# Softmax weights that leave PSUM before they are split, with reciprocals, padded values and matmul order rearranged

## The chip, the cores and the metric

The kernel runs on one core of a Trainium2 chip. The metric is the device time of one execution in microseconds (us). Three runs of the kernel before gave 1035.32 (median), 1034.66 and 1037.95 us.

Engines are named as the profile names them: PE (TensorE, matmuls), PEld (its weight loads), DVE (VectorE), ACT (ScalarE), POOL (GpSimd) and SP (SyncE, which here issues DMAs). Each takes its instructions in one fixed order.

## The reference, cut to what matters

Attention over 8 batches, 12 heads, 448 positions, 64 channels, followed by a gated MLP per batch with a spatial matmul over positions:

```python
q_n, k_n = rmsnorm(q, g_q), rmsnorm(k, g_k)
scores = q_n @ k_n.T / 8
attn = exp(scores - max(scores))
attn = attn / (sum(attn) + 1e-9)
x = attn @ v                          # (8, 448, 768) after merging heads
h = gelu_tanh(x @ w_in)               # 768 -> 1024, w_in and w_out are float64
u, v = h[..., :512], h[..., 512:]
v_n = (v - mean(v)) / sqrt(var(v) + 1e-6) * g_ln
v_s = einsum('ts,bsd->btd', w_sg, v_n) + b_sg[None, :, None]
out = x + (u * v_s) @ w_out
```

## The kernel before, in words

To keep float32 accuracy on float16 matmuls, most operands are split into a high and a low part: the high part is a cast, the low part the value less the cast, and a product takes three matmuls (high by high, low by high, high by low).

**Turns.** The program is written as 48 turns, one for a pair of heads (i; six of them make a batch b). Two pairs form a unit u. In a unit, `scores(u)` handles seven tiles of 128 query rows for two heads each. For a tile: matmuls into a PSUM buffer `s` (L389, two buffers of two banks, `ps_s`), the negated row maximum on DVE (`nm`, L392), two exponentials on ACT in place in PSUM, which also write the row sums (L394), a copy to float16 on ACT (`ahl`, L397), the low part by a subtraction on DVE that reads PSUM and the copy (L398), and a DMA transpose into `at` (L403), the softmax weights with keys on partitions. The `s` buffer is free for the scores two tiles later when the subtraction is done. `ahl` has three buffers.

**One turn behind**, `pv(i)` makes the output of a pair: `recips(i)` forms the reciprocals of the row sums (add on POOL L413, reciprocal on DVE L414, cast to `rh` and low part `rl` on POOL L415 and L416), spreads them over partitions with 16 small matmuls (`row`, L423) and copies them out of PSUM (L426). Then 24 matmuls multiply `v` (split by `vsplit` on ACT and DVE, L369 and L370) with `at` (L446), in three pieces between which other work is put. 448 positions are 3.5 tiles of 128, so the fourth tile of a head fills half of the partitions; both heads of a pair share it, and its matmuls run as 64-by-64 tiles of PE's array. The output is scaled (L450) and split into `xh` and `xl` (L453, L454).

**MLP.** `moe(b)` is a generator that the turns of the next batch advance: the matmuls for the `v` half (L510, L513), the gelu, the layer norm, the `u` half (L568), the spatial matmul (L598: for each of four 128-column pieces f, nine matmuls over full tiles and three over the half tile, whose rows lie on one half of the partitions for f 0 and 1 and on the other for f 2 and 3), the gate (DVE L603, POOL L604, L607, L608), and the output matmuls (L632, L636, L638, L644). Weights are decoded from float64 in the first two batches' turns (L152 to L158, L241 to L247).

**POOL** also normalises and splits q and k of the units ahead (L329, L330, L335).

**What sets the order.** Streams (scores, pv, weights, moe) are interleaved by shares: in a turn `scores` gets SC steps, `pv` SV steps, `moe` its M steps, each step being the code up to the next `yield`. On top of that the framework's scheduler places the instructions of each engine by priority and by its own simulated time line, so that the built order is not the written one.

Of the kernel before, what the change touches and what calls it, by code (L numbers as in the profile page):

```python
# [34 lines left out]
SC, SV = 7, 4  # L35
# [11 lines left out]
def kernel(  # L47
# [236 lines left out]
    VR = {}  # L284

    def load_v(i):
# [6 lines left out]
        vr = ld.tile([P, GV, C7, D], F32, name="vr", bufs=NVR)  # L293
# [2 lines left out]
        for h, half, s0, c0, n in ((0, lo, 0, 0, C4), (0, hi, 0, C4, CM), (1, lo, C4, C4, CM), (1, hi, CM, 0, C4)):
# [76 lines left out]
    at_all = att.tile([P, 2 * C7, NAT * S], F16, name="at", bufs=1)  # L373

    def scores(u):
# [5 lines left out]
        for t in range(C7):  # L381
# [10 lines left out]
            V.tensor_reduce(out=nm, in_=ps[:, :, 0:S], axis=AX.X, op=ALU.max, negate=True)  # L392
            for h in range(2):
                A.activation(out=ps[:, h, 0:S], in_=ps[:, h, 0:S], func=AF.Exp, bias=nm[:, h:h + 1], accum_out=sums[:, t, h:h + 1])  # L394
# [2 lines left out]
            A.activation(out=ahl[:, 0], in_=ps[:, :, 0:S], func=AF.Copy)  # L397
            V.tensor_tensor(out=ahl[:, 1], in0=ps[:, :, 0:S], in1=ahl[:, 0], op=ALU.subtract)  # L398
# [7 lines left out]
    def recips(i):  # L406

        u, j = divmod(i, NG)
        cs = slice(0, C4) if j == 0 else slice(CM, C7)
# [3 lines left out]
        G.tensor_scalar(out=x, in0=sums, scalar1=1e-9, scalar2=None, op0=ALU.add)  # L413
# [1 line left out]
        G.tensor_copy(out=rh, in_=y)  # L415
        G.tensor_tensor(out=rl, in0=y, in1=rh, op=ALU.subtract)  # L416
        ps = ps_v.tile([P, 512], F32, name="row", tag="pv")[:, 0:S]
        for n, t in enumerate(range(cs.start, cs.stop)):
            ks, o = (slice(0, P), t * P - j * S) if t != CM else ((lo, SM), (hi, 0))[j]
            for rx in (rh, rl):  # L420
                for h in range(2):
                    w = ks.stop - ks.start
                    mm(out=ps[h * HP:(h + 1) * HP, o:o + w], lhsT=rx[ks, 2 * n + h:2 * n + h + 1].broadcast_to([w, HP]),  # L423
                       rhs=ident_h[ks, ks], start=(n == 0 and rx is rh), stop=(n == CM and rx is rl), skip_group_check=True)
# [6 lines left out]
    def pv(i):  # L431
# [12 lines left out]
        for k_, (vx, n, hx) in enumerate(blocks):  # L444
# [347 lines left out]
```

## Time and profile before

| | |
|---|---|
| median of 3 runs | 1035.32 us (1034.66 to 1037.95) |
| profiled execution, span | 1033.44 us, 1031.6 us |
| mean granted clock of PE | 0.916 |
| DMA moved | 155.70 MB, queue q1 69.0% of 16 engines |
| scores (L389) | 1152 matmuls in 168 tiles |
| subtractions (L398) | 168, 182.1 us of DVE |
| spatial matmuls (L598) | 384, of which 96 over half of the rows |

Busy shares are averages over stretches with different limits, so the stretches are read one by one: to 250 us the weights are decoded beside the first turns, from 250 to 960 us attention and MLP run together, and the last 72 us hold the last MLP alone. A wait row reads "engine, tile and line that waited, the one that ended the wait: us in total, times, longest".

### The profile page before, as it was taken

To read this page: it belongs to the slowest core of one execution; us is meant where nothing else is said; L and a number is where in the kernel's file an instruction comes from. 1 tells how busy PE (TensorE), PEld (TensorE's weight loads), DVE (VectorE), ACT (ScalarE), POOL (GpSimd) and SP (SyncE) were. 2 spreads that over 40 slices of the span, in tenths; PEclk is the share of its full clock that TensorE was granted. 3 is DMA by queue.
4 is the path that set the end of the run, shared out by engine and by line. 5 is a ranking of instruction groups with operands and counts; after the bars stand their busy time and mean duration, and the time that the engine had idled before them with its cause. 6 is when DMAs were issued, how large, how long until landed. Compare 5 with 4: busy or idle time off the path is not lost.

```text
span 1031.6 us, 16639 instructions
## 1 busy us (share of the span) xinstructions
PE 829.0 (80%) x5844; PEld 421.1 (41%) x5844; DVE 733.3 (71%) x1332; ACT 738.1 (72%) x1449; POOL 386.9 (38%) x403
## 2 busy tenths in 40 slices
PE   0243666858798997899689998999779998998798
PEld 0111222324444563346234553446324563454246
DVE  6698888999587667786677758786669666766230
ACT  3767779877868767777768767987777776877351
POOL 1468614567253505243251606341533414030021
PEclk9976687969899999999699998999889999999899
DMA  6998748776886398478886488959967676556102
GB/s 163 214 228 191 166 115 196 185 176 130 181 197 150 88 204 180 98 170 145 186 175 147 99 194 183 182 123 176 194 142 160 141 166 125 106 135 123 40 1 62
DMA packets 448004, 155.70 MB, mean 151 GB/s; under 512 B 404336, under 2 KB 441776, under 8 KB 447920
## 3 DMA queue, kind: packets, MB, share of 16 engines
q1 hardware_dynamic: 447344, 154.18, 69.0%
q8 instruction: 46, 0.75, 0.3%
q10 hardware_dynamic: 576, 0.46, 0.2%
q14 instruction: 38, 0.31, 0.1%
HBM read 43.57 MB, written 11.01 MB: 53 GB/s over the span
## 4 chain that ended last, share of the span: by engine, by line
PE 34%; DVE 21%; ACT 19%; DMA 11%; issue 8%; SPq 4%; POOL 4%; ACTq 0%; POOLq 0%; DVEq 0%
PE pv L446 6%; ACT s L394 5%; DVE ahl L398 5%; PE s L389 4%; DVE nm L392 3%; ACT ahl L397 2%; DMA vr<-in_v_dram 2%; ACT sqk L308 2%; DMA raw<-in_moe_w_in_dram 2%; DMA at<-ahl 2%; POOL qk L330 2%; DMA qt<-hl 2%; DMA qk<-in_k_dram 2%; ACT hl L334 2%; SPq L336 1%
## 5 line engine op out<-in xcount | busy, mean ns | idle before, releaser
L394 ACT ACTIVATE s<-s,nm 128x448 f32<-128x448 f32 x336 | 204.0, 607 | 109.8 <-DVE nm L392 106.8
L398 DVE TENSOR_TENSOR ahl<-s,ahl 128x896 f16<-128x896 f32 x168 | 182.1, 1085 | 100.8 <-ACT ahl L397 99.8
L389 PE MATMUL s<-qt 64*128 64x448 f16 (+1 forms) x1152 | 143.2, 390 | 110.7 <-DVE ahl L398 76.4
L392 DVE TENSOR_REDUCE nm<-s 128x2 f32<-128x896 f32 x168 | 180.8, 1082 | 40.5 <-PE s L389 40.0
L397 ACT ACTIVATE ahl<-s 128x896 f16<-128x896 f32 x168 | 153.4, 920 | 5.3 <-DMA at<-ahl 3.1
L446 PE MATMUL pv<-at,vh 128*64 128x448 f16 (+1 forms) x768 | 122.7, 398 | 16.4 <-DMA at<-ahl 7.6
L413 POOL TENSOR_SCALAR rx<-sums 128x8 f32<-128x8 f32 x48 | 13.4, 278 | 311.8 <-ACT s L394 310.4
L389 PEld LDWEIGHTS <-qt 64*128 64x128 f16 (+1 forms) x1152 | 45.3, 102 | 177.2 <-issue 135.9
L330 POOL TENSOR_TENSOR qk<-qk,ny 128x896 f32<-128x896 f32 x46 | 80.8, 1774 | 85.8 <-DVE ny L125 82.3
L335 POOL TENSOR_TENSOR hl<-qk,hl 128x896 f16<-128x896 f32 x46 | 87.7, 1917 | 55.1 <-ACT hl L334 54.5
L568 PEld LDWEIGHTS <-wi 128*128 128x128 f16 x576 | 55.9, 100 | 60.2 <-issue 14.1
L446 PEld LDWEIGHTS <-vh 128*64 128x64 f16 (+1 forms) x768 | 43.4, 117 | 84.3 <-issue 70.2
L309 DVE TENSOR_REDUCE ss<-sqk 128x14 f32<-128x896 f32 x48 | 51.8, 1080 | 29.2 <-ACT sqk L308 28.9
L394 ACT ACTIVATION_READ_ACCUMULATOR s<-s,nm 128x1 f32 x336 | 67.7, 201 | 0.0
L329 POOL TENSOR_TENSOR qk<-qk,gg 128x896 f32<-128x896 f32 x23 | 48.0, 2085 | 43.2 <-ACT sqk L308 39.3
L423 PE MATMUL row<-ident_h,rh 128*64 128x128 f16 (+1 forms) x384 | 36.7, 240 | 31.7 <-POOL rh L415 24.0
L604 POOL TENSOR_TENSOR gt<-gt,u 128x448 f32<-128x448 f32 x32 | 38.5, 1206 | 60.1 <-DVE gt L603 55.9
L446 PE MATMUL pv<-at,vl 128*64 128x448 f16 (+1 forms) x384 | 60.4, 394 | 0.0
L334 ACT ACTIVATE hl<-qk 128x896 f16<-128x896 f32 x48 | 44.9, 947 | 15.9 <-POOL qk L330 8.4
L308 ACT ACTIVATE sqk<-qk 128x896 f32<-128x896 f32 x48 | 45.6, 951 | 8.2 <-DVE ss L309 4.4
L510 PEld LDWEIGHTS <-xh 128*128 128x128 f16 x288 | 27.0, 101 | 49.2 <-issue 21.9
L369 ACT ACTIVATE vh<-vr,v_s 128x448 f16<-128x448 f32 x48 | 31.9, 668 | 19.7 <-PE pv L446 19.6
(996 smaller groups left out, 1960.8 us busy)
## 6 DMA issues: line engine op xcount, KB each, us to landing
out_dram<-ot SPq DMA_DIRECT2D x56, 192.0 KB, 2.9
vr<-in_v_dram SPq DMA_DIRECT2D x32, 192.0 KB, 3.3
raw<-in_moe_w_in_dram SPq DMA_DIRECT2D x12, 512.0 KB, 5.7
qk<-in_q_dram SPq DMA_DIRECT2D x47, 128.0 KB, 2.8
qk<-in_k_dram SPq DMA_DIRECT2D x47, 128.0 KB, 2.8
vr<-in_v_dram SPq DMA_DIRECT2D x32, 144.0 KB, 3.3
qk<-in_q_dram SPq DMA_DIRECT2D x47, 96.0 KB, 2.6
qk<-in_k_dram SPq DMA_DIRECT2D x47, 96.0 KB, 2.6
```

Of the source, the lines that this page charges most:

```text
L308: A.activation(out=skv, in_=U[u]["qk"][:, x].rearrange("p h c d -> p (h c) d"), func=AF.Square)
L309: V.tensor_reduce(out=SS[u][:, x], in_=skv, axis=AX.X, op=ALU.add)
L330: E.tensor_tensor(out=qk, in0=qk, in1=r["rs"][:, x * SSW:(x + 1) * SSW].unsqueeze(2).broadcast_to([P, SSW, D]), op=ALU.mult)
L334: A.activation(out=h_, in_=r["qk"][:, x], func=AF.Copy)
L335: E.tensor_tensor(out=l_, in0=r["qk"][:, x], in1=h_, op=ALU.subtract)
L389: mm(out=ps[r_, h, 0:S], lhsT=qt[hs, qx, t * P + r_.start:t * P + r_.stop], rhs=qt[hs, kx, j * S:(j + 1) * S], start=(m == 0), stop=(m == 2))
L392: V.tensor_reduce(out=nm, in_=ps[:, :, 0:S], axis=AX.X, op=ALU.max, negate=True)
L394: A.activation(out=ps[:, h, 0:S], in_=ps[:, h, 0:S], func=AF.Exp, bias=nm[:, h:h + 1], accum_out=sums[:, t, h:h + 1])
L397: A.activation(out=ahl[:, 0], in_=ps[:, :, 0:S], func=AF.Copy)
L398: V.tensor_tensor(out=ahl[:, 1], in0=ps[:, :, 0:S], in1=ahl[:, 0], op=ALU.subtract)
L446: mm(out=ps[h * HP:(h + 1) * HP], lhsT=vx[ks, c], rhs=at_all[ks, n + c, o:o + S], start=(k_ == 0), stop=(k_ == len(blocks) - 1), skip_grou ...
L568: done = mm(out=ps[:, 0:S], lhsT=ww[:, g, f * P:(f + 1) * P], rhs=xx, start=(n == 0), stop=(n == 17))
```

## The change

- **Exponentials** (L394, now L429) write a new float32 tile `ex` in SBUF (two buffers) instead of PSUM in place. Copy (now L432) and subtraction (now L433) read `ex`. PSUM's `s` is free after the exponentials. `ahl` has two buffers instead of three.
- **Reciprocals**: the add, the cast and the low part move from POOL to DVE (now L387 to L390) and are written in `scores`, right behind the fourth and the seventh tile. `pv` only does the row matmuls (now L403) and their copy (`recip_row`, L406).
- **`pv`** starts with a `yield`, and does rows, matmuls and the split in one step; SV goes from 4 to 3.
- **v** is stored in eight columns of 64 instead of seven, with zeros where a half tile has nothing; so the shared fourth tile takes three full matmuls (now L454) instead of six 64-by-64 ones. The copies, squares and splits of v go over 512 columns instead of 448.
- **`moe`**: the steps of the half tile of `x @ w_in` have no `yield` between them; the spatial matmul is written for f 0 and 2 together, then 1 and 3, with the half-tile matmuls of the two (now L615) taking turns.

```diff
-SC, SV = 7, 4
+SC, SV = 7, 3
-NAT, NAH, NQT, NVH, HLB, GV = 3, 3, 2, 2, 3, 3
-NOT, NX = 2, 12
+NAT, NAH, NQT, NVH, HLB, GV = 3, 2, 2, 2, 3, 3
+NOT, NX, NEX = 2, 12, 2
...
+    C8 = C7 + 1
+    vr_all = [ld.tile([P, GV, C8, D], F32, name=f"vr{n}", bufs=1) for n in range(NVR)]
+    for x in vr_all:
+        G.memset(x[hi, :, CM], 0.0)
+        G.memset(x[lo, :, C4], 0.0)
...
-            for h in range(2):
-                A.activation(out=ps[:, h, 0:S], in_=ps[:, h, 0:S], func=AF.Exp, bias=nm[:, h:h + 1], accum_out=sums[:, t, h:h + 1])
+            ex = att.tile([P, 2, S], F32, name="ex", bufs=NEX)
+            for h in range(2):
+                A.activation(out=ex[:, h], in_=ps[:, h, 0:S], func=AF.Exp, bias=nm[:, h:h + 1], accum_out=sums[:, t, h:h + 1])
             yield
             ahl = att.tile([P, 2, 2, S], F16, name="ahl", bufs=NAH)
-            A.activation(out=ahl[:, 0], in_=ps[:, :, 0:S], func=AF.Copy)
-            V.tensor_tensor(out=ahl[:, 1], in0=ps[:, :, 0:S], in1=ahl[:, 0], op=ALU.subtract)
+            A.activation(out=ahl[:, 0], in_=ex, func=AF.Copy)
+            V.tensor_tensor(out=ahl[:, 1], in0=ex, in1=ahl[:, 0], op=ALU.subtract)
...
+            if t in (CM, C7 - 1):
+                recips(NG * u + (t > CM))
...
-        G.tensor_scalar(out=x, in0=sums, scalar1=1e-9, scalar2=None, op0=ALU.add)
+        V.tensor_scalar(out=x, in0=sums, scalar1=1e-9, scalar2=None, op0=ALU.add)
         V.reciprocal(out=y, in_=x)
-        G.tensor_copy(out=rh, in_=y)
-        G.tensor_tensor(out=rl, in0=y, in1=rh, op=ALU.subtract)
+        V.tensor_copy(out=rh, in_=y)
+        V.tensor_tensor(out=rl, in0=y, in1=rh, op=ALU.subtract)
...
-        row = recips(i)
         yield
+        row = recip_row(i)
         ps = ps_v.tile([P, 512], F32, name="pv")[:, 0:S]
+        parts = ((vh, 0), (vl, 0), (vh, C7))
+        for k_, (vx, n) in enumerate(parts):
+            mm(out=ps, lhsT=vx[:, CM:CM + 2].rearrange("p c d -> p (c d)"), rhs=at_all[:, n + CM, o:o + S],
+               start=(k_ == 0), stop=False, skip_group_check=True)
+        for c in range(CM):
+            for vx, n in parts:
+                for h in range(2):
+                    mm(out=ps[h * HP:(h + 1) * HP], lhsT=vx[:, c + h * (C4 + 1)], rhs=at_all[:, n + c + h * C4, o:o + S],
+                       start=False, stop=(c == CM - 1 and n == C7), skip_group_check=True)
...
-            if st % 2 == 1:
+            if st % 2 == 1 and (early or t != CM or g == NP - 1):
                 yield
...
+        for f0 in range(2):
+            psf = {f: ps_m.tile([P, 512], F32, name="ms_", tag="mm") for f in (f0, f0 + 2)}
+            for f, ps in psf.items():
+                n = 0
+                for t in range(CM):
+                    o = t * DH + f * P
+                    for vx, wx in ((vh, ws_h), (vh, ws_l), (vl, ws_h)):
+                        mm(out=ps[:, 0:S], lhsT=vx[:, o:o + P], rhs=wx[:, t], start=(n == 0), stop=False)
+                        n += 1
+                yield
+
+            for n, (vx, wx) in enumerate(((vh, ws_h), (vh, ws_l), (vl, ws_h))):
+                for f, ps in psf.items():
+                    p0, o = f // 2 * HP, CM * DH + f0 * P
+                    mm(out=ps[:, 0:S], lhsT=vx[p0:p0 + HP, o:o + P], rhs=wx[p0:p0 + HP, CM], start=False, stop=(n == 2))
```

How the built order moves, at three places.

PE, the end of a spatial matmul in the second batch's MLP. Before, two pieces of one accumulation `ms` (full tiles, then the half tile) and then the output matmuls:

```order
L598 MATMUL ms__3565<-ws_h,vl 128x448
L598 LDWEIGHTS vh
L598 MATMUL ms__3565<-ws_h,vh 128x448
L598 LDWEIGHTS vh
L598 MATMUL ms__3565<-ws_l,vh 128x448
L598 LDWEIGHTS vl
L598 MATMUL ms__3565<-ws_h,vl 128x448
L632 LDWEIGHTS xh
```

and after the change, where L615 are the half-tile matmuls:

```order
L608 MATMUL ms__3536<-ws_h,vl 128x448
L615 LDWEIGHTS vh
L615 MATMUL ms__3536<-ws_h,vh 128x448
L615 LDWEIGHTS vh
L615 MATMUL ms__3536<-ws_l,vh 128x448
L615 LDWEIGHTS vl
L615 MATMUL ms__3536<-ws_h,vl 128x448
L647 LDWEIGHTS xh
```

The code has the half-tile matmuls of two accumulations take turns; in the built order the three of one accumulation (here `ms__3536`) still follow each other, and its partner's stand elsewhere. It is so for all 96.

PE, scores beside the output matmuls of the half tile, after the change (before, the twelve or more score matmuls of a tile, which fall in pairs for two heads, mostly stand together):

```order
L423 LDWEIGHTS qt
L423 MATMUL s<-qt 128x448
L651 LDWEIGHTS xt
L651 MATMUL mo__3872<-idn,xt 64x128
L423 LDWEIGHTS qt
L423 MATMUL s<-qt 128x448
L653 LDWEIGHTS xl
L653 MATMUL mo__3872<-idn,xl 64x128
```

Here single score matmuls stand between others, away from the partner for the other head.

DVE, attention in the middle of the run (`nm` are the maxima, `ahl` the subtractions, `rx`, `ry`, `rh`, `rl` the reciprocals). Before:

```order
L398 TENSOR_TENSOR ahl<-s,ahl 128x896
L392 TENSOR_REDUCE nm<-s 128x2
L414 RECIPROCAL ry<-rx 128x8
L398 TENSOR_TENSOR ahl<-s,ahl 128x896
L392 TENSOR_REDUCE nm<-s 128x2 x2
L398 TENSOR_TENSOR ahl<-s,ahl 128x896 x2
L392 TENSOR_REDUCE nm<-s 128x2
```

and after:

```order
L387 TENSOR_SCALAR rx<-sums 128x8
L388 RECIPROCAL ry<-rx 128x8
L433 TENSOR_TENSOR ahl<-ex,ahl 128x896
L389 CAST rh<-ry 128x8
L390 TENSOR_TENSOR rl<-ry,rh 128x8
L426 TENSOR_REDUCE nm<-s 128x2 x2
L433 TENSOR_TENSOR ahl<-ex,ahl 128x896
L314 TENSOR_REDUCE ss<-sqk 128x14
L426 TENSOR_REDUCE nm<-s 128x2
```

Before, at most two maxima stand ahead of the subtraction of the oldest tile; after, three do at 39 places and four at 7, and the three reciprocal steps that POOL had are DVE's.

More of the change, by code (lines that the diff above doesn't have):

```diff
@@ L292, in load_v @@
         b, g = divmod(i, NP)
[L293 removed]
+        vr = vr_all[i // GV % NVR]
         vp = vr.rearrange("p g c d -> p g (c d)")
         src = v[b, 2 * g:2 * (g + GV)].rearrange("(g h) (p c) d -> h p g (c d)", h=2, c=C7)
[L296 removed]
+        for h, half, s0, c0, n in ((0, lo, 0, 0, C4), (0, hi, 0, C4, CM), (1, lo, C4 + 1, C4, CM), (1, hi, C4, 0, C4)):
             nc.sync.dma_start(out=vp[half, :, s0 * D:(s0 + n) * D], in_=src[h][:, :, c0 * D:(c0 + n) * D])
@@ L365, in vsplit @@
         sc = VS[i // NP]["sc"]
-        vh, vl = (att.tile([P, C7, D], F16, name="v" + c, bufs=NVH) for c in "hl")
+        vh, vl = (att.tile([P, C8, D], F16, name="v" + c, bufs=NVH) for c in "hl")
         vr = VR.pop(i)
@@ L373, with recips, recip_row @@
     at_all = att.tile([P, 2 * C7, NAT * S], F16, name="at", bufs=1)
+    def recips(i):
+        u, j = divmod(i, NG)
+        cs = slice(0, C4) if j == 0 else slice(CM, C7)
+        sums = U[u]["sums"][:, cs].rearrange("p t h -> p (t h)")
+        x, y = (sml.tile([P, 2 * C4], F32, name=f"r{c}", bufs=2) for c in "xy")
+        U[u]["r", j] = rh, rl = [sml.tile([P, 2 * C4], F16, name=f"r{c}", bufs=3) for c in "hl"]
+        V.tensor_scalar(out=x, in0=sums, scalar1=1e-9, scalar2=None, op0=ALU.add)
+        V.reciprocal(out=y, in_=x)
+        V.tensor_copy(out=rh, in_=y)
+        V.tensor_tensor(out=rl, in0=y, in1=rh, op=ALU.subtract)
+    def recip_row(i):
+        u, j = divmod(i, NG)
+        cs = slice(0, C4) if j == 0 else slice(CM, C7)
+        rh, rl = U[u]["r", j]
+        ps = ps_v.tile([P, 512], F32, name="row", tag="pv")[:, 0:S]
+        for n, t in enumerate(range(cs.start, cs.stop)):
+            ks, o = (slice(0, P), t * P - j * S) if t != CM else ((lo, SM), (hi, 0))[j]
+            for rx in (rh, rl):
+                for h in range(2):
+                    w = ks.stop - ks.start
+                    mm(out=ps[h * HP:(h + 1) * HP, o:o + w], lhsT=rx[ks, 2 * n + h:2 * n + h + 1].broadcast_to([w, HP]),
+                       rhs=ident_h[ks, ks], start=(n == 0 and rx is rh), stop=(n == CM and rx is rl), skip_group_check=True)
+        row = att.tile([P, S], F32, name="row", bufs=1)
+        A.activation(out=row, in_=ps, func=AF.Copy)
+        return row
     def scores(u):
@@ L588, in moe @@
         bb = W["bb"]
-        for f in range(FT):
-            ps = ps_m.tile([P, 512], F32, name="ms_", tag="mm")
-            n = 0
-            for t in range(CK):
-                p0, p1, o = 0, P, t * DH + f * P
-                if t == CM:
-                    p0 = f // 2 * HP
-                    p1, o = p0 + HP, t * DH + f % 2 * P
-                for vx, wx in ((vh, ws_h), (vh, ws_l), (vl, ws_h)):
-                    mm(out=ps[:, 0:S], lhsT=vx[p0:p1, o:o + P], rhs=wx[p0:p1, t], start=(n == 0), stop=(n == 11))
-                    n += 1
-                if t == 1:
-                    yield
-            gt = mlp.tile([P, S], F32, name="gt", tag="gt", bufs=NOT)
-            V.scalar_tensor_tensor(out=gt, in0=ps[:, 0:S], scalar=W["gw"][:, f:f + 1], in1=bb, op0=ALU.mult, op1=ALU.add)
-            G.tensor_tensor(out=gt, in0=gt, in1=u[f], op=ALU.mult)
-            A.activation(out=gh[:, f], in_=gt, func=AF.Copy)
-            gl.append(mlp.tile([P, S], F32R, name="gl", tag="ug", bufs=5))
-            G.tensor_tensor(out=gl[f], in0=gt, in1=gh[:, f].bitcast(F32), op=ALU.subtract)
-            G.tensor_tensor(out=gtl[:, f, half], in0=gt[:, SM:S], in1=gh[:, f, SM:S].bitcast(F32), op=ALU.subtract)
```

40 lines of the change are left out of this document (11 added, 29 removed).

## The prediction

> **What bounds the kernel now.** I read the page's busy shares first, then the chain of waits, then the busy time of three stretches, then the waits. The median of the runs is 1035.3 us. The profiled execution took 1033.4 us with a span of 1031.6, so 1.8 us lie outside the span, and it stands 0.2% under the median; the sum below is made against 1033.4. Busy shares and the chain, from the page:
>
> ```profile
> span 1031.6 us, 16639 instructions
> PE 829.0 (80%) x5844; PEld 421.1 (41%) x5844; DVE 733.3 (71%) x1332; ACT 738.1 (72%) x1449; POOL 386.9 (38%) x403
> ...
> PE 34%; DVE 21%; ACT 19%; DMA 11%; issue 8%; SPq 4%; POOL 4%; ACTq 0%; POOLq 0%; DVEq 0%
> PE pv L446 6%; ACT s L394 5%; DVE ahl L398 5%; PE s L389 4%; DVE nm L392 3%; ACT ahl L397 2%; DMA vr<-in_v_dram 2%; ACT sqk L308 2%; DMA raw<-in_moe_w_in_dram 2%; DMA at<-ahl 2%; POOL qk L330 2%; DMA qt<-hl 2%; DMA qk<-in_k_dram 2%; ACT hl L334 2%; SPq L336 1%
> ```
>
> No engine is the bound of the whole. The stretches differ (columns: stretch, its length, busy us and count of PE, PEld, DVE, ACT, POOL, granted clock, DMA share, GB/s):
>
> ```profile
> 50.00:250.00 200.00, 122.07 (x784) 52.27 (x784) 183.68 (x318) 154.76 (x300) 115.05 (x95) 0.76 0.76 172
> 250.00:960.00 710.00, 636.10 (x4641) 328.77 (x4640) 504.58 (x917) 533.22 (x1065) 246.38 (x275) 0.95 0.73 154
> 960.00:1032.00 72.00, 61.39 (x360) 36.00 (x360) 14.93 (x40) 24.52 (x39) 10.67 (x15) 0.95 0.12 29
> ```
>
> From 50 to 250 us VectorE is busy 184 of 200 us: what is added to it there lengthens the run. From 250 to 960 TensorE is busy 636 of 710, with VectorE at 71% and ScalarE at 75%: there TensorE's waits and work count most. The waits that the change touches, first over the whole run, then (last four rows) from 250 to 960 alone:
>
> ```profile
> PE s L389 <- DVE ahl L398: 76.4, 35, 9.0
> PE row L423 <- POOL rh L415: 24.0, 13, 5.3
> POOL rx L413 <- ACT s L394: 310.4, 31, 21.5
> ...
> PE s L389 <- DVE ahl L398: 21.2, 22, 3.0
> PE row L423 <- POOL rh L415: 16.5, 9, 5.3
> DVE ahl L398 <- ACT ahl L397: 86.9, 74, 3.8
> ACT s L394 <- DVE nm L392: 88.2, 48, 6.0
> ```
>
> Of the 76.4 us in which scores wait for the subtraction to leave PSUM, 55 lie outside the late stretch, where TensorE has time to spare.
>
> **The change, part by part.** (1) *Reciprocals.* All four of their instructions now stand on VectorE, right behind the scores that they need, while the row matmuls come a turn later. TensorE's 24.0 us of waiting for rh have no cause left. I take the 16.5 of the late stretch; bounds 0 (something else is late at that place) and 24.0. POOL no longer stands 310 us behind the exponentials; that is idle time of an engine off the path, priced at nothing.
>
> (2) *Early release of PSUM.* Scores of a tile two further on now wait for the exponentials instead of for copy and subtraction. By TensorE's waits this is worth 21.2 us in the late stretch; by the chain, copy and subtraction are 7% of the span, 72 us, of which the half that leads back to scores (the other half leads to the transposes) is 36. I take 30. Bounds 0 and 76.4.
>
> (3) *TensorE's work.* Spacing of matmuls, by their starts:
>
> ```profile
> 349.08 0.35 PE L598 MATMUL ms__3565<-ws_l,vh 128*128 128x448 f16 x1
> 349.27 0.35 PE L598 MATMUL ms__3565<-ws_h,vl 128*128 128x448 f16 x1
> 349.55 0.36 PE L598 MATMUL ms__3565<-ws_h,vh 64*128 64x448 f16 x1
> 349.75 0.35 PE L598 MATMUL ms__3565<-ws_l,vh 64*128 64x448 f16 x1
> 349.94 0.35 PE L598 MATMUL ms__3565<-ws_h,vl 64*128 64x448 f16 x1
> 350.23 0.23 PE L632 MATMUL mo__3651<-idn,xh 128*128 128x128 bf16 x1
> ```
>
> One of 448 columns takes 0.19 us, and 0.28 to 0.29 where the tile shape changes. The spatial matmuls are written in pairs on two halves of the rows; if a pair ran as one, 48 x 0.19 = 9.1 us would go. But in the order as built none of the 96 half-row matmuls stands next to its partner: the three of one f come in a row, as before (the first place shown above). So this saves nothing. Instead 36 score matmuls more than before (616 against 580 of 1152) have lost their partner's neighbourhood: 36 x 0.19 = 6.8. Changes of shape stay, 763 to 759. The zero-padded centre takes three matmuls in place of three pairs, which is no time, and drops a few changes of shape at that place. I take +5; bounds -9.1 and +10.
>
> (4) *VectorE and ScalarE, direct.* Durations (rows of the groups by form, and four of single lines with min/median/max ns):
>
> ```profile
> L398 DVE TENSOR_TENSOR ahl<-s,ahl 128x896 f16<-128x896 f32 x168 | 182.1, 1085 | 100.8 <-ACT ahl L397 99.8 <-issue 0.3
> L397 ACT ACTIVATE ahl<-s 128x896 f16<-128x896 f32 x168 | 153.4, 920 | 5.3 <-DMA at<-ahl 3.1
> L334 ACT ACTIVATE hl<-qk 128x896 f16<-128x896 f32 x48 | 44.9, 947 | 15.9 <-POOL qk L330 8.4 <-DVE qk L330 7.2
> L394 ACT ACTIVATE s<-s,nm x336: 578/608/656, 25.3 to 960.0; 128x448 f32<-128x448 f32 x168
> L577 ACT ACTIVATE u<-mu__2093,hs x1: 634/634/634, 228.9 to 228.9; 128x448 f32<-128x448 f32 x1
> L201 DVE TENSOR_TENSOR wi<-tmp,wi x6: 1208/1216/2703, 127.3 to 146.4; 128x1024 f16<-128x1024 f32 x6
> L317 DVE TENSOR_SCALAR nx<-ss x24: 165/179/1977, 11.7 to 854.1; 128x28 f32<-128x28 f32 x24
> ```
>
> VectorE gets 144 small instructions at 0.18 us (L317's median) = 26, and 64 more columns in each vl, 4 more: 30 us. The subtraction itself, undisturbed, stays: L201, from SBUF, takes 1.21 us for 1024, so 1.06 for 896, against 1.09 from PSUM. ScalarE: an exponential that writes SBUF costs as L577, 634 against 608, x336 = 8.7; a copy that reads SBUF as L334, 947 against 920, x168 = 4.5; padding some 3; together 16.
>
> (5) *Waiting for POOL.* This is the price that speaks against the change. A VectorE instruction with both inputs in SBUF that starts while POOL is running is held until POOL is done:
>
> ```profile
> 227.24 5.23 DVE L556 TENSOR_TENSOR vl<-vg,vh 128x512 f16<-128x512 f32 x4
> ...
> 227.35 4.23 POOL L330 TENSOR_TENSOR qk<-qk,ny 128x896 f32<-128x896 f32 x2
> ...
> L370 DVE SCALAR_TENSOR_TENSOR vl<-vr,v_s,vh x48: 651/676/2030, 41.6 to 943.0; 128x448 f16<-128x448 f32 x48
> L398 DVE TENSOR_TENSOR ahl<-s,ahl x168: 1027/1091/1093, 30.8 to 961.7; 128x896 f16<-128x896 f32 x168
> ```
>
> Four L556 that take 2.5 us alone took 5.2 beside POOL, and L370 reaches 2.03. L398, which reads PSUM, never passes 1.093 in 168 times: today it is free of this, and with ex in SBUF it is not. Laying its starts against POOL's rows, without the reciprocals that go, 46 of the 168 start inside one, with 31.5 us of it still to run; 13 of the 46, with 10.6 us, are among the 33 subtractions before 250 us. The first and the last of the 46:
>
> ```profile
> 27.62 3.71 POOL L335 TENSOR_TENSOR hl<-qk,hl 128x896 f16<-128x896 f32 x2
> 30.78 1.09 DVE L398 TENSOR_TENSOR ahl<-s,ahl 128x896 f16<-128x896 f32 x1 [4.53 <-ACT ahl L397]
> ...
> 913.37 1.52 POOL L604 TENSOR_TENSOR gt<-gt,u 128x448 f32<-128x448 f32 x1 [2.99 <-DVE gt L603]
> 914.77 1.09 DVE L398 TENSOR_TENSOR ahl<-s,ahl 128x896 f16<-128x896 f32 x1 [0.36 <-ACT ahl L397]
> ```
>
> The four reciprocal steps can be held too: L317 has a median of 0.179 and a maximum of 1.977. One hold per group at an estimated 0.27 us, x48 = 13; bounds 0 and 39. Behind a held subtraction stand the next maxima, and ScalarE's exponentials wait for these.
>
> The Trainium skill (SBUF — State Buffer, Who interferes with whom) says that a VectorE instruction with two SBUF inputs and a GpSimd instruction that reads SBUF exclude each other for their whole length. The trace agrees (5.23 against 2.5 us above). Were there no such rule, the sum below would lack its terms for holds and come to 1010.
>
> (6) *Two ahl buffers instead of three.* A copy now waits until the transpose two tiles earlier has landed:
>
> ```profile
> at<-ahl SPq DMA_TRANSPOSE x176, 3.7
> ```
>
> With 3.7 us to landing, 10 of the copies at today's times would start too early, by 18 us together; bounds 0 and, if tiles come closer together, twice that.
>
> **The sum.** Before 250 us VectorE's additions count in full: direct 6 (a fifth of 30, as 33 of 168 tiles fall there), holds 10.6 + 2, together +19. After it they count with VectorE's 21% of the chain: (24 + 20.9 + 11) x 0.21 = +12; ScalarE's late 13 and the 18 of (6) with its 19%: +6. So 1033.4 - 16.5 - 30 + 5 + 19 + 12 + 6 = 1028.9. I forecast **1029 us**, a little faster, 0.6% under the median.
>
> **Rivals.** *A, much better (12%).* The release is worth the chain's whole 72 us: 1033.4 - 16.5 - 72 + 42 = 987. For it: VectorE and ScalarE wait for each other 175 us in the late stretch, and the new order puts three maxima in a row. Against it: TensorE idles only 74 us there.
> *B, no difference (18%).* TensorE's waits only change their name: with the release worth the 21.2 alone the sum is 1038, and with half of the late holds absorbed 1034; I take 1036.
> *C, slower by the holds (24%).* The subtraction waits for POOL, and VectorE sets the pace late too. Half of its late 56 lands instead of a fifth, and the release gives 21.2: 1033.4 - 16.5 - 21.2 + 5 + 19 + 28 + 6 = 1054. It decides from where holds exceed 60 us. For it: VectorE is at 92% early. Against: 205 us of idle VectorE late. The Trainium skill's rule above is what this rival rests on besides the rows.
> *D, slower by the buffers (10%).* Bursts of three maxima make bursts of copies, and 36 us of ScalarE's standing for transposes land for half, 18 instead of 3: 1029 + 15 = 1044.
> That the paired matmuls don't pair is not a rival but read from the order, and in the sum.
>
> **How the numbers follow.** My forecast has 36%, with a range of its own of 1010 to 1032. A difference under 0.3% (3 us) a measurement here can't tell from none. Faster: 36 + 12 = 48%; same: B's 18%; slower: 24 + 10 = 34%. The range runs from 996 (which leaves out most of A) to 1056 (which leaves out under half of C).
>
> **What would show it.** Right: TensorE's waits for rh gone; scores waiting for exponentials, not for the subtraction; the subtraction with a median of about 1.09 us but a maximum near 3 and a sum of 205 to 230 us instead of 182; half-row spatial matmuls still 0.19 us apart. Wrong: a subtraction that stays at 1.09 throughout (no holds, and 1010 is nearer), VectorE's busy time above 830 us (C), copies waiting over 20 us for transposes (D), or half-row matmuls starting in pairs.

## The result, and the profile after

The changed kernel takes 1025.89 us (median of four runs, 1023.31 to 1028.16); four runs of the kernel before beside it have a median of 1036.3. The ratio is 0.9899, with a 95% interval of 0.9868 to 0.9929: about 1% faster. The profiled execution took 1023.31 us with a span of 1021.5, against 1033.44 and 1031.6 before. The forecast was 1029.

First the page's busy shares and its chain, as shown of before:

```profile
span 1021.5 us, 16315 instructions
PE 826.5 (81%) x5700; PEld 423.3 (41%) x5700; DVE 801.4 (78%) x1476; ACT 739.6 (72%) x1449; POOL 385.4 (38%) x263
...
DVE 31%; PE 28%; ACT 16%; DMA 10%; issue 9%; POOL 3%; SPq 3%; ACTq 0%; DVEq 0%; POOLq 0%
```

VectorE has 68 us more work (801.4 against 733.3), and the chain that ended last now lies on it for 31% instead of 21%. TensorE's work is the same. POOL lost 140 instructions and almost no busy time. The time by stretch (columns as in the prediction):

```profile
50.00:250.00 200.00, 109.58 (x711) 47.61 (x708) 186.56 (x328) 154.05 (x300) 97.57 (x59) 0.76 0.73 165
250.00:960.00 710.00, 650.77 (x4591) 336.23 (x4589) 572.56 (x1053) 538.78 (x1071) 262.50 (x174) 0.96 0.74 157
960.00:1022.00 62.00, 56.45 (x342) 35.23 (x340) 11.75 (x35) 21.78 (x33) 10.07 (x12) 1.00 0.10 26
```

To 250 us nothing is won: VectorE is busy 187 of 200 us there, and TensorE gets through 711 matmuls where it did 784 (the change leaves 144 of 5844 out in all). The gain lies between 250 and 960, with TensorE busy 651 instead of 636. The waits: the first row is of the kernel before, the next four of the changed one over the whole run, and the last four of it from 250 to 960 alone:

```profile
PE row L423 <- DVE xl L454: 2.7, 1, 2.7
...
PE s L423 <- ACT ex L429: 62.4, 30, 7.7
ACT ahl L432 <- DMA at<-ahl: 35.8, 31, 3.3
PE row L403 <- DVE xl L465: 30.4, 11, 8.9
PE row L403 <- DVE rh L389: 9.4, 3, 7.4
...
PE s L423 <- ACT ex L429: 12.2, 14, 1.7
ACT ex L429 <- DVE nm L426: 42.8, 34, 4.1
PE row L403 <- DVE xl L465: 7.5, 5, 3.3
PE row L403 <- DVE rh L389: 0.4, 1, 0.4
```

Late, scores wait 12.2 us for the exponentials where they waited 21.2 for the subtraction, and the exponentials wait 42.8 for maxima instead of 88.2. ScalarE now stands 35.8 us for transposes. The row matmuls still wait: late 7.9 in place of 16.5, over the whole run 39.8 for these two in place of 24.0 for `rh` and 2.7 for `xl`. Most of it is now for `xl` (L465), the last reader of the output of the pair before; rows and output of a pair share one PSUM buffer (`ps_v`, tag `pv`), so reciprocals that are ready don't let the rows start.

VectorE's subtraction by its line (count, min/median/max in ns, first and last start in us):

```profile
L433 DVE TENSOR_TENSOR ahl<-ex,ahl x168: 1040/1091/2777, 31.5 to 939.6; 128x896 f16<-128x896 f32 x168
```

and the groups of VectorE that the change adds, lengthens or moves to SBUF (busy us, mean ns, then idle time before):

```profile
L433 DVE TENSOR_TENSOR ahl<-ex,ahl 128x896 f16<-128x896 f32 x168 | 213.4, 1272 | 56.8 <-ACT ahl L432 55.4
L375 DVE SCALAR_TENSOR_TENSOR vl<-vr,v_s,vh 128x512 f16<-128x512 f32 x48 | 49.7, 1039 | 1.3 <-ACT vh L374 1.0
L390 DVE TENSOR_TENSOR rl<-ry,rh 128x8 f16<-128x8 f32 x48 | 18.1, 376 | 0.7
L389 DVE CAST rh<-ry 128x8 f16<-128x8 f32 x48 | 17.9, 374 | 0.6
L387 DVE TENSOR_SCALAR rx<-sums 128x8 f32<-128x8 f32 x48 | 16.8, 349 | 11.8 <-ACT ex L429 11.4
```

The subtraction has kept its median (1.09 us) and has got a tail to 2.78: 213.4 us in sum, 31 more than 182.1. The three small steps of the reciprocals take 0.35 to 0.38 us on average, 52.8 us in sum. The split of v takes 49.7 us instead of 36.6. Together that is 97 us more, over the 68 of the page: other groups of VectorE got shorter, and in the trace the records of neighbouring instructions overlap in part.

The subtraction's first and last start also tell how far attention is: the last one starts at 939.6 us, against 961.7 before. So attention ends 22.1 us sooner, but what follows is longer, 81.9 us (1021.5 less 939.6) instead of 69.9, since more of the MLP is left by then (436 of its matmuls start after that, against 314). More than half of the gain is given back at the end.

### The profile page after: what moved, and what is told of

Same layout as the page of the kernel before. It is cut to its first block, busy times and chain, and to the rows that moved or that the text cites. A ratio compares the mean times of both kernels' runs of the same rounds, so it can differ in the third digit from the quotient of the medians.

```text
span 1021.5 us, 16315 instructions
## 1 busy us (share of the span) xinstructions
PE 826.5 (81%) x5700; PEld 423.3 (41%) x5700; DVE 801.4 (78%) x1476; ACT 739.6 (72%) x1449; POOL 385.4 (38%) x263
## 4 chain that ended last, share of the span: by engine, by line
DVE 31%; PE 28%; ACT 16%; DMA 10%; issue 9%; POOL 3%; SPq 3%; ACTq 0%; DVEq 0%; POOLq 0%
DVE ahl L433 8%; DMA at<-ahl 5%; DVE nm L426 5%; ACT ex L429 5%; ACT ahl L432 3%; PE s L423 3%; PE pv L459 3%; DVE vl L375 2%; DMA vr<-in_v_dram 2%; DVE ss L314 2%; DVE vl L568 1%; ACT sqv L358 1%; DVE pv L461 1%; DMA raw<-in_moe_w_in_dram 1%; SPq L302 1%
## 5 line engine op out<-in xcount | busy, mean ns | idle before, releaser
L429 ACT ACTIVATE ex<-s,nm 128x448 f32<-128x448 f32 x336 | 209.4, 631 | 76.8 <-DVE nm L426 51.6
L433 DVE TENSOR_TENSOR ahl<-ex,ahl 128x896 f16<-128x896 f32 x168 | 213.4, 1272 | 56.8 <-ACT ahl L432 55.4
L423 PE MATMUL s<-qt 64*128 64x448 f16 (+1 forms) x1152 | 156.9, 389 | 88.7 <-ACT ex L429 62.4
L432 ACT ACTIVATE ahl<-ex 128x896 f16<-128x896 f32 x168 | 159.7, 951 | 37.8 <-DMA at<-ahl 35.8
L340 POOL TENSOR_TENSOR hl<-qk,hl 128x896 f16<-128x896 f32 x46 | 94.6, 2070 | 69.9 <-ACT hl L339 69.7
L459 PE MATMUL pv<-at,vh 128*64 128x448 f16 x576 | 91.8, 371 | 0.0
L580 PEld LDWEIGHTS <-wi 128*128 128x128 f16 x576 | 57.6, 104 | 72.6 <-issue 31.3
L403 PE MATMUL row<-ident_h,rh 128*64 128x128 f16 (+1 forms) x384 | 36.6, 241 | 39.9 <-DVE xl L465 30.4
L429 ACT ACTIVATION_READ_ACCUMULATOR ex<-s,nm 128x1 f32 x336 | 67.8, 202 | 0.0
L459 PE MATMUL pv<-at,vl 128*64 128x448 f16 x288 | 53.2, 367 | 0.0
L375 DVE SCALAR_TENSOR_TENSOR vl<-vr,v_s,vh 128x512 f16<-128x512 f32 x48 | 49.7, 1039 | 1.3 <-ACT vh L374 1.0
L459 PEld LDWEIGHTS <-vh 128*64 128x64 f16 x576 | 33.7, 114 | 40.5 <-issue 23.4
L403 PEld LDWEIGHTS <-rh 128*64 128x64 f16 (+1 forms) x384 | 22.5, 117 | 61.9 <-DVE xl L465 34.6
```

Of the source, the lines that this page charges most:

```text
L340: E.tensor_tensor(out=l_, in0=r["qk"][:, x], in1=h_, op=ALU.subtract)
L375: V.scalar_tensor_tensor(out=vl.rearrange("p c d -> p (c d)"), in0=vr, scalar=sc, in1=vf, op0=ALU.mult, op1=ALU.subtract)
L423: mm(out=ps[r_, h, 0:S], lhsT=qt[hs, qx, t * P + r_.start:t * P + r_.stop], rhs=qt[hs, kx, j * S:(j + 1) * S], start=(m == 0), stop=(m == 2))
L429: A.activation(out=ex[:, h], in_=ps[:, h, 0:S], func=AF.Exp, bias=nm[:, h:h + 1], accum_out=sums[:, t, h:h + 1])
L432: A.activation(out=ahl[:, 0], in_=ex, func=AF.Copy)
L433: V.tensor_tensor(out=ahl[:, 1], in0=ex, in1=ahl[:, 0], op=ALU.subtract)
```

## The experiments

Times are medians in us; ratios are to the kernel before on the same chip, with 95% intervals. "Undo" runs take one part out of the changed kernel, "only" runs put one part into the kernel before.

| run | us | ratio |
|---|---|---|
| the change | 1025.89 | 0.9899 [0.9868, 0.9929] |
| exponentials in place in PSUM again | 1065.68 | 1.0286 [1.0264, 1.0307] |
| reciprocals on POOL again | 1013.64 | 0.976 [0.971, 0.981] |
| before's MLP loop | 1021.09 | 0.9847 [0.9823, 0.9871] |
| before's `pv` in three pieces | 1017.57 | 0.9808 [0.9781, 0.9836] |
| only the exponentials to SBUF | 1005.29 | 0.9705 [0.9675, 0.9734] |
| only the reciprocals on DVE | 1044.8 | 1.0082 [1.0055, 1.011] |
| exponentials to SBUF, reciprocals early on POOL | 1006.68 | 0.9715 [0.9697, 0.9733] |
| the change, POOL's low parts replaced by a zero fill | 1015.19 | 0.9789 [0.9754, 0.9824] |
| only exponentials, larger MLP share | 1022.03 | 0.9884 [0.9826, 0.9941] |
| only exponentials, three `ahl` buffers | 1014.72 | 0.979 [0.9752, 0.9828] |
| only exponentials, one `ex` buffer | 1042.14 | 1.0057 [1.0035, 1.0078] |
| only exponentials, 11 `xh`/`xl` buffers | 1005.16 | 0.9716 [0.9686, 0.9747] |

### One part undone at a time

**Exponentials.**

```diff
-NAT, NAH, NQT, NVH, HLB, GV = 3, 2, 2, 2, 3, 3
+NAT, NAH, NQT, NVH, HLB, GV = 3, 3, 2, 2, 3, 3
-            A.activation(out=ahl[:, 0], in_=ex, func=AF.Copy)
-            V.tensor_tensor(out=ahl[:, 1], in0=ex, in1=ahl[:, 0], op=ALU.subtract)
+            A.activation(out=ahl[:, 0], in_=ps[:, :, 0:S], func=AF.Copy)
+            V.tensor_tensor(out=ahl[:, 1], in0=ps[:, :, 0:S], in1=ahl[:, 0], op=ALU.subtract)
```

(and the exponentials write `ps` again.)

> The changed kernel with the exponentials in place in PSUM again, the subtraction reading PSUM, and three ahl buffers; all other parts of the change stay. Theory (the early release of PSUM is the larger part of the gain, worth some 30 us, and the holds behind POOL take back about half of it): 1030 to 1038 us, scores waiting for the subtraction again, late waits of scores back from 12 to 20 us or more, and no subtraction over 1.1 us. Rival (the holds cost as much as the release gives, and the gain comes from other parts): 1015 to 1027 us.

Measured: 1065.68, 39.8 us above the change and 2.9% above the kernel before, and far above both expected ranges. The run has three `ahl` buffers again, as the kernel before has. Two waits of this kernel:

```profile
PE s L423 <- DVE ahl L432: 73.1, 38, 8.0
PE row L403 <- DVE rh L389: 23.3, 8, 9.1
```

and its subtraction (ns as above):

```profile
L432 DVE TENSOR_TENSOR ahl<-s,ahl x168: 1026/1091/1094, 31.3 to 993.2; 128x896 f16<-128x896 f32 x168
```

The subtraction from PSUM is again never longer than 1.094 us, and scores wait for it as before. Undoing it costs far more than the whole change gains, so the other parts together are a loss. That the subtraction is held goes with its source in SBUF.

**Reciprocals.**

```diff
-        V.tensor_scalar(out=x, in0=sums, scalar1=1e-9, scalar2=None, op0=ALU.add)
+        G.tensor_scalar(out=x, in0=sums, scalar1=1e-9, scalar2=None, op0=ALU.add)
-        V.tensor_copy(out=rh, in_=y)
-        V.tensor_tensor(out=rl, in0=y, in1=rh, op=ALU.subtract)
+        G.tensor_copy(out=rh, in_=y)
+        G.tensor_tensor(out=rl, in0=y, in1=rh, op=ALU.subtract)
```

> The changed kernel with the add, the cast and the low part of the reciprocals on POOL again, still written right behind the scores. Theory (moving them behind the scores, not moving them to VectorE, frees the row matmuls; on VectorE they cost 53 us of busy time with holds): 1018 to 1027 us, VectorE busy near 750 us instead of 801. Rival (POOL standing behind the exponentials in its order delays q and k): 1030 us or more, with POOL waiting over 200 us for ACT.

Measured: 1013.64 (four runs from 1003.91 to 1016.05), 12.3 faster than the change and below the range of the theory. Busy shares and the subtraction's group from its page:

```profile
PE 830.0 (82%) x5700; PEld 426.6 (42%) x5700; DVE 770.1 (76%) x1332; ACT 737.7 (73%) x1449; POOL 437.6 (43%) x407
...
L433 DVE TENSOR_TENSOR ahl<-ex,ahl 128x896 f16<-128x896 f32 x168 | 223.7, 1333 | 67.6 <-ACT ahl L432 66.9
```

and the rows' wait:

```profile
PE row L403 <- DVE xl L465: 28.3, 10, 8.3
```

VectorE has 31 us less to do, although its subtractions take longer in sum (223.7; POOL is busier too, 437.6 us for 385.4). The reciprocals are still written right behind the scores here, so the 12.3 us are for the engine alone. The rows wait for `xl` about as long as with the reciprocals on VectorE (28.3 and 30.4).

**The MLP's order, and `pv`.**

```diff
-            if st % 2 == 1 and (early or t != CM or g == NP - 1):
+            if st % 2 == 1:
...
-        for f0 in range(2):
-            psf = {f: ps_m.tile([P, 512], F32, name="ms_", tag="mm") for f in (f0, f0 + 2)}
+        for f in range(FT):
+            ps = ps_m.tile([P, 512], F32, name="ms_", tag="mm")
...
```

> The changed kernel with the spatial matmul written one f after the other and the yields of the half tile as before. Theory (the pairs never stand together in the built order, so the edit gives nothing): 1023 to 1030 us. Rival (pairing or the missing yields pay): 1033 us or more.

```diff
-SC, SV = 7, 3
+SC, SV = 7, 4
...
+        blocks = blocks[CM::C4] + [x for n, x in enumerate(blocks) if n % C4 != CM]
+        row = recip_row(i)
         yield
-        row = recip_row(i)
...
+            if k_ in (4, 8):
+                yield
...
-        yield
```

(eight columns of v and early reciprocals stay.)

> The changed kernel with the output matmuls in three pieces, the shared tile as six 64-by-64 matmuls, and four steps, as before; padded v and early reciprocals stay. Theory (it is the release that lets attention run ahead; this part is worth under 6 us): 1023 to 1032 us. Rival (one block a step later is what drew the scores together): 1034 us or more.

Measured: 1021.09 and 1017.57, 4.8 and 8.3 faster than the change, both below the ranges of their theories, which had these parts at next to nothing. The first is small: its interval touches the change's own. So the `pv` edit as a whole costs, and nothing shows that the new order of the spatial matmuls gains. Which of the things inside the `pv` edit costs (one step instead of three, its place in the turn, or full matmuls in place of half ones) was not separated.

### One part alone

```diff
-NOT, NX = 2, 12
+NOT, NX, NEX = 2, 12, 2
+            ex = att.tile([P, 2, S], F32, name="ex", bufs=NEX)
-                A.activation(out=ps[:, h, 0:S], in_=ps[:, h, 0:S], func=AF.Exp, bias=nm[:, h:h + 1], accum_out=sums[:, t, h:h + 1])
+                A.activation(out=ex[:, h], in_=ps[:, h, 0:S], func=AF.Exp, bias=nm[:, h:h + 1], accum_out=sums[:, t, h:h + 1])
```

(on the kernel before; copy and subtraction read `ex`, `ahl` has two buffers.)

> The kernel before with one part of the change alone: exponentials to SBUF, copy and subtraction from there, two ahl buffers. Theory after the first four runs (the early release is the whole gain, and the other parts cost): 995 to 1018 us, attention over 20 us or more earlier, held subtractions as after the change. Rival (the release pays only together with reciprocals that are ready early): 1024 us or more.

Measured: 1005.29, 31.4 under the kernel before and 20.6 under the change, within the range of the theory. **With this part alone the kernel is faster than with the whole change**; the two other fastest runs below (1005.16 and 1006.68) contain it too and are no different from it. Two of its stretches:

```profile
50.00:250.00 200.00, 119.71 (x790) 51.14 (x790) 185.33 (x312) 154.64 (x306) 112.08 (x88) 0.78 0.75 171
250.00:960.00 710.00, 662.11 (x4779) 346.91 (x4778) 531.06 (x960) 542.91 (x1084) 300.09 (x285) 0.98 0.72 156
```

its subtraction:

```profile
L399 DVE TENSOR_TENSOR ahl<-ex,ahl x168: 1034/1092/2964, 31.6 to 911.3; 128x896 f16<-128x896 f32 x168
```

Late, TensorE is busy 662 of 710 us, and the last subtraction starts 50.4 us sooner than before. To 250 us TensorE gets through 790 matmuls, 6 more than before. Its waits:

```profile
PE s L389 <- ACT ex L395: 54.0, 33, 10.4
ACT ex L395 <- DVE nm L392: 48.9, 40, 5.2
ACT ahl L398 <- DMA at<-ahl: 42.4, 40, 2.8
PE row L424 <- DVE xl L455: 22.3, 12, 7.1
```

The reciprocals are POOL's again and written a turn later, right before the rows, and yet the rows wait for `xl` here too, and only 2.4 us for `rh`. By the trace a pair's rows start 9 us after its `rh` is done (median of 48), 1.8 us in the kernel before: attention is further ahead of the rows, and the PSUM buffer is what is late.

```diff
+            if t in (CM, C7 - 1):
+                recips(NG * u + (t > CM))
...
-        row = recips(i)
+        row = recip_row(i)
```

(on the kernel before, with the reciprocals on VectorE in one run; on the run with `ex` alone, with them on POOL, in the other.)

> The kernel before with the reciprocals' four instructions on VectorE behind the scores, and nothing else. Theory (on VectorE they cost more than the row matmuls' wait for rh was worth): 1036 to 1055 us. Rival (the prediction's first term, 16.5 us of waiting saved against some 15 paid): 1025 to 1035 us.

> The kernel before with two parts: exponentials to SBUF (two ahl buffers), and the reciprocals behind the scores but all on POOL save the reciprocal itself. Theory (it keeps what paid and leaves out what cost): 990 to 1013 us, the fastest so far. Rival (the parts left out carry some of the gain): 1014 to 1026 us.

Measured: 1044.8 (8 slower than the kernel before) and 1006.68 (no different from 1005.29), both within the ranges of their theories. Rows' wait of the first:

```profile
PE row L398 <- DVE rh L384: 20.7, 8, 4.8
```

and of the second:

```profile
PE row L398 <- DVE xl L463: 22.3, 11, 7.1
```

Writing the reciprocals a turn earlier is worth nothing. On POOL it costs nothing; on VectorE it costs 8 to 12. What costs is that they stand on VectorE. And the first run still waits 20.7 us for `rh` where the kernel before waited 24.0: without the exponentials' edit the rows wait for `rh` whichever engine makes it.

### The price of waiting for POOL

```diff
-            E.tensor_tensor(out=l_, in0=r["qk"][:, x], in1=h_, op=ALU.subtract)
+            (E.tensor_tensor(out=l_, in0=r["qk"][:, x], in1=h_, op=ALU.subtract) if E is V else G.memset(l_, 0.0))
```

> The changed kernel with POOL's subtraction that makes the low parts of q and k (46 instructions, 95 us of POOL) replaced by a fill with zeros on POOL, which reads nothing; the low parts of q and k are left out of the result. Theory (VectorE's holds behind POOL are on the path late with about a fifth of their length): subtractions' sum from 213 down to 190 to 203 us, the time down by 3 to 12 us. Rival C of the prediction (holds set the pace): down by more than 15 us. If fills hold VectorE as well, the sum stays above 208.

Measured: 1015.19, 10.7 under the change. Busy shares from its page, and two groups of VectorE:

```profile
PE 832.4 (82%) x5700; PEld 426.5 (42%) x5700; DVE 777.8 (77%) x1476; ACT 739.1 (73%) x1449; POOL 329.9 (32%) x263
...
L433 DVE TENSOR_TENSOR ahl<-ex,ahl 128x896 f16<-128x896 f32 x168 | 205.6, 1226 | 50.7 <-ACT ahl L432 49.8
...
L375 DVE SCALAR_TENSOR_TENSOR vl<-vr,v_s,vh 128x512 f16<-128x512 f32 x48 | 46.4, 972 | 3.2 <-ACT vh L374 3.1
```

VectorE's busy time falls by 23.6 us without one instruction less on it, the subtractions by 7.8 and the split of v by 3.3. So POOL's work does lengthen VectorE's, and swapping 46 of its operations for a fill moves the time. The time lies in the range of the theory; the subtractions' 205.6 us lie above its 190 to 203. Their trace says why: in the changed kernel only 8 subtractions start beside these 46 and are held, for 6.9 us in sum. A fill does not hold them: 7 subtractions start during one in this run and take 1.08 to 1.09 us. The 10.7 is a bound for the price of their holds, not the price: those operations also stood on the way to q and k.

### What the exponentials' edit lives on

Three runs on the kernel with `ex` alone, and a fourth that one of them called for.

```diff
-WR, M0, M1, MR, ML = 3, 8, 7, 11, 11
+WR, M0, M1, MR, ML = 3, 8, 8, 13, 13
```

> Exponentials to SBUF alone (1005 us), with more of each turn's steps given to the MLP (shares 7, 11, 11 become 8, 13, 13). Theory (with the release attention ends 52 us earlier but the MLP is left behind, and 21 of them are given back in a last stretch of 92 us that TensorE fills): last stretch 75 to 85 us, 990 to 1002 us. Rival (the MLP lags because TensorE is full, not because of its share): 1003 to 1012 us, attention ending later by what the end gains.

Measured: 1022.03 (three runs within 1021.6 and 1022.3, one at 1034.33), 16.7 slower and above both expected ranges. Its subtraction:

```profile
L399 DVE TENSOR_TENSOR ahl<-ex,ahl x168: 1036/1092/2953, 31.3 to 936.9; 128x896 f16<-128x896 f32 x168
```

and its late stretch:

```profile
250.00:960.00 710.00, 650.82 (x4654) 340.16 (x4653) 541.17 (x927) 533.43 (x1068) 293.80 (x284) 0.95 0.73 156
```

What follows the last subtraction does get shorter, from 89.1 to 83.2 us (span 1020.1), but attention ends 25.6 later. The theory that the MLP is merely left behind by too small a share falls: with a larger share, attention loses more than the end saves. TensorE's late busy time falls with it (651 for 662). The order on VectorE and ScalarE also differs from the 408th instruction on, so the share and the order that the scheduler makes of it are not separated.

```diff
-NAT, NAH, NQT, NVH, HLB, GV = 3, 2, 2, 2, 3, 3
-NOT, NX, NEX = 2, 12, 2
+NAT, NAH, NQT, NVH, HLB, GV = 3, 3, 2, 2, 3, 3
+NOT, NX, NEX = 2, 11, 2
```

> Exponentials to SBUF alone, with three ahl buffers as before the change (and eleven xh and xl buffers instead of twelve, to make room). Theory (copies waiting 42 us for transposes count with ScalarE's share of the chain): waits for transposes under 10 us, 994 to 1004 us. Rival (ScalarE's wait is hidden, or comes back behind the maxima): 1003 to 1010 us.

```diff
-NOT, NX, NEX = 2, 12, 2
+NOT, NX, NEX = 2, 11, 2
```

> The kernel before with only the exponentials' edit, two ahl buffers, and 11 buffers of xh and xl instead of 12 (a batch's MLP reads 6 of them; the next batch's are written meanwhile). The run with three ahl buffers (1014.7 us against 1005.3) had 11 of these too, since the space was needed, so two causes stand open for its 9.4 us. Theory: it is the third ahl buffer, which lets copies run ahead and moves the standing from the transposes (42.4 to 8.5 us) to the maxima (48.9 to 74.2): then this run stays within 1002 to 1009, with 35 to 50 us of copies waiting for transposes. Rival: it is the missing xh/xl buffer, which holds up the output of a pair and with it the rows behind it: then this run comes near 1015, with more waiting of the copies of the output for the MLP's matmuls. A run in between leaves both in, or says that any edit of this size moves the built order by so much.

Measured: 1014.72 with the third `ahl` buffer (above both ranges), 1005.16 with the smaller NX alone (within the theory's). Waits with three `ahl` buffers:

```profile
ACT ex L395 <- DVE nm L392: 74.2, 54, 5.2
PE s L389 <- ACT ex L395: 71.5, 30, 9.9
...
ACT ahl L398 <- DMA at<-ahl: 8.5, 8, 2.6
```

and with two, and 11 buffers of `xh` and `xl`:

```profile
PE s L389 <- ACT ex L395: 56.4, 32, 10.3
ACT ex L395 <- DVE nm L392: 48.5, 42, 5.2
ACT ahl L398 <- DMA at<-ahl: 41.3, 38, 3.2
```

NX is innocent. The third buffer does take the waits for transposes away (41.3 to 8.5), and the kernel is 9.6 us slower for it: exponentials stand for the maxima and scores for the exponentials instead. Its built order also differs nearly everywhere, so whether the buffer or the order that it leads the scheduler to is to blame stays open. What is shown is that taking 33 us of ScalarE's waiting away made nothing faster.

```diff
-NOT, NX, NEX = 2, 12, 2
+NOT, NX, NEX = 2, 12, 1
```

> Exponentials to SBUF alone, with one ex buffer instead of two: PSUM is still free after the exponentials, but the next tile's exponentials wait for this tile's subtraction. Theory (what pays is PSUM free early, so that scores and maxima go ahead): below the kernel before by 8 us or more, 1006 to 1028 us. Rival (what pays is that ScalarE no longer stands behind VectorE's subtraction): 1035 us or more, near the kernel before or above it.

Measured: 1042.14, 0.6% above the kernel before, in the range of the rival. Its waits:

```profile
ACT ex L395 <- DVE ahl L399: 106.2, 90, 3.7
PE s L389 <- ACT ex L395: 86.4, 37, 12.3
```

PSUM is still released by the exponentials here, two tiles ahead as in the change. But the exponentials of a tile wait for the subtraction of the tile before, and the gain is gone. So releasing PSUM early didn't pay here without a second place to put the exponentials, so that ScalarE goes on while VectorE is still splitting. What the early release is worth by itself this run doesn't show: one `ex` buffer ties the exponentials closer to the subtraction than PSUM did, which had two, and the 106.2 us that they wait for it are a wait that the kernel before doesn't have. The built order also differs nearly everywhere from that of the run with two.

## Why the prediction came out as it did

1025.89 lies 3 us under the forecast of 1029, inside its own range and with the forecast sign. But the terms that made it were wrong in both directions, and their errors cancel: that the number is close is luck.

**Early release, step (2) with its costs: much too small.** The sum gave it −30, and against that 10.6 of early holds, 4.4 of late ones (20.9 × 0.21) and some 6 on ScalarE (with the two `ahl` buffers): −9 net. Measured: −31.4 alone, −39.8 in company of the rest. The step that failed is its sizing by the rows of TensorE's waits and half of the chain's 72 us. ScalarE's late wait for maxima (88.2) was left out of the sum, as only rival A counted on it; it fell to 42.8. The step also looked for its gain in the late stretch alone; with `ex` alone attention is already 7 us ahead at 250 us (below). The run with one `ex` buffer says that the name of the step was too narrow as well: PSUM is released early there too, and nothing is gained. By the prediction's terms `ex` alone would come to 1033.4 − 9 = 1024, and with rival A's 72 in place of the 30 to 982; it came to 1005, halfway between.

**Reciprocals, step (1) with its part of (4) and (5): wrong sign.** −16.5 for the rows against some +14 (26 us direct and 13 of holds, early in full, late with 21%): −2.6 net. Measured: +8 alone, and in the change +12.3 for VectorE in place of POOL. The step that failed is that the 24.0 us of waiting for `rh` "have no cause left". POOL was not what made `rh` late. In the kernel before, POOL stood waiting for the last exponential in 31 of 48 pairs (the 310.4 us of the prediction's rows), as here at 270 us (start and duration in us; in brackets the engine's idle time and what ended it):

```profile
270.11 0.21 ACT L394 ACTIVATION_READ_ACCUMULATOR s<-s,nm 128x1 f32 x1
270.40 0.24 POOL L413 TENSOR_SCALAR rx<-sums 128x8 f32<-128x8 f32 x1 [10.25 <-ACT s L394]
271.31 0.19 POOL L415 CAST rh<-ry 128x8 f16<-128x8 f32 x1 [0.67 <-DVE ry L414]
271.55 0.32 PE L423 MATMUL row<-ident_h,rh 128*64 128x128 f16 x2 [2.93 <-POOL rh L415]
```

By the traces `rh` is done 1.5 us after the pair's last exponential in the kernel before (median of 48 pairs), 2.1 with the reciprocals alone on VectorE and 2.7 in the change. They come no earlier for being written earlier, since the exponentials come no earlier: TensorE's wait for `rh` was in the main a wait for the exponentials, and it stays (20.7) as long as these stay in PSUM. With the exponentials in SBUF it goes, with the reciprocals on POOL too (2.4 with `ex` alone); but the rows also need the PSUM buffer of the pair before, and wait for `xl` instead (30.4 in the change, 22.3 with `ex` alone). The run with the reciprocals early on POOL, 1006.68, has all of that step and none of its gain. Also, 13 us for holds in the reciprocals was too little, as the three steps take 52.8 where 144 at their median of 0.166 would take 24.

**VectorE early counts in full: in part at most.** The sum put +19 there and no gain. The 36th tile's first exponential starts at 256.6 before and at 258.0 after, 1.4 us later. With the reciprocals back on POOL it starts at 252.0, so they cost 6 in the change, near the 7 that the sum gave them; with the reciprocals alone on VectorE it starts at 256.5, and they cost nothing. With `ex` alone it starts at 249.7, 7 us sooner than before, although the subtractions are held there (10.9 us in sum before 250 us, by the trace). So the exponentials' edit gains early as well, more than its holds cost there.

**Holds, step (5): right in place and size for the subtraction.** Forecast 31.5 us for the subtraction, a median of 1.09 with a maximum near 3 and a sum of 205 to 230; measured 31, 1.091, 2.777 and 213.4. (In the other runs with the exponentials in SBUF it was 24 to 46 us by the traces, so that it hit so closely is in part chance.) The Trainium skill (SBUF — State Buffer, Who interferes with whom) states that a VectorE instruction with two SBUF inputs contends with a GpSimd instruction that reads SBUF. The trace agrees: from PSUM no subtraction passes 1.094 us, from SBUF they reach 2.96. Rival C rested on holds of over 60 us in all; they came to some 70 (31 in subtractions, 29 in the reciprocals, 10 in v's split; VectorE's 801 us stay under C's mark of 830), but the release outweighed them: C's other half, a release worth 21.2, was wrong.

**TensorE's work, step (3): +5, with `pv` at nothing.** The half-tile matmuls don't pair, as read from the order. In the changed kernel three of one accumulation still follow each other 0.2 us apart (min/median/max in ns, first and last start in us):

```profile
L615 PE MATMUL ms__3433<-ws_h,vh x1: 360/360/360, 354.8 to 354.8; 64*128 64x448 f16 x1
L615 PE MATMUL ms__3433<-ws_l,vh x1: 349/349/349, 355.0 to 355.0; 64*128 64x448 f16 x1
L615 PE MATMUL ms__3433<-ws_h,vl x1: 349/349/349, 355.2 to 355.2; 64*128 64x448 f16 x1
```

Going back to the old loop gives 4.8 us, near the 5, but not shown to be by the reason given (scores that lose their partner). In the order of their starts 8 of the 1152 scores have no other score next to them before, 55 in the change and 64 in the run with `ex` alone, and that is the fastest of the three. In the `pv` edit the padded centre was priced as no time, and `pv` in one block has no term at all; together they cost 8.3.

**Two `ahl` buffers, step (6): the cost is not seen.** The sum gave it +3 (18 us at 19%). Copies wait 35.8 us for transposes, over the 20 that were to be the mark of D. But with `ex` alone, where they wait 41.3, a third buffer takes the wait away and the kernel is 9.6 us slower, so a wait of that size is no sign of D. It also means that the −31.4 of `ex` alone holds for two `ahl` buffers; with three it is −22.1 (1014.72 against 1036.79). Whether that comes from the buffer or from the order that goes with it stays open; in the changed kernel itself it was not tried.

Taken one at a time, the parts come to −31.4 + 12.3 + 4.8 + 8.3 = −6 with the exponentials as measured alone, and to −14.4 with the −39.8 measured in the change. The whole is −10.4, in between: roughly additive.

## What to carry to other kernels

Before a wait is counted as a gain, look up what the late thing was itself waiting for, and what else is needed at that place: here the reciprocals had stood behind the exponentials, and behind them stood a PSUM buffer. Where a pipeline of three engines shares one PSUM buffer, ask what each extra buffer lets which engine do ahead; here a second SBUF copy between two engines was worth 37 us over a single one, while the kernel with one more buffer behind it was slower. And when a change has several parts, time each by itself: here one part was worth 3%, and the others gave two thirds of that back.

## What was not expected of the hardware

- Instructions of eight columns are held as well. The add, the cast and the subtraction of the reciprocals have medians of 0.166 to 0.170 us and maxima of 1.65 to 1.82, so that holds more than double their cost; the cast and the add have one input only. All 34 that take over 0.23 us overlap an instruction of POOL; a cast at 88.04 us, for one, ends at 89.47, and POOL's at 89.44:

```profile
L387 DVE TENSOR_SCALAR rx<-sums x48: 154/166/1697, 39.8 to 938.6; 128x8 f32<-128x8 f32 x48
L389 DVE CAST rh<-ry x48: 156/170/1652, 42.5 to 939.1; 128x8 f16<-128x8 f32 x48
```

- Holds work both ways, it seems: POOL's low parts of q and k, which no edit touched, take 2.07 us on average in the changed kernel and 1.92 before. No run took this apart.
- The granted clock of the late stretch went up with the faster kernels: 0.95 before, 0.96 after, 0.98 with `ex` alone, though TensorE was busier. By the trace's clock record TensorE had half speed for 72 us of that stretch before, 58 after and 34 with `ex` alone; in the changed kernel the starts of the `u` half's matmuls (L580, 448 columns) lie 0.373 us apart there and 0.189 elsewhere. The clock isn't the whole gain: the run with the larger MLP share has 0.95, as the kernel before, and is 14.8 us under it. How much of the gain of `ex` alone came with the clock (19 us at most, an estimate: half of 72 less 34), and whether the clock rose because the waits went, no run separates.
